# Attention and a two-layer network on one core: batch 0's plain values loaded as four tokens a partition and moved into place by TensorE

## The chip, the core and the metric

The kernel runs on one core of a Trainium2 chip. The metric is the device time of one execution in microseconds; lower is better. Its engines are PE (TensorE, matrix products), ACT (ScalarE), DVE (VectorE), POOL (GpSimd) and SP (SyncE, which here issues nearly all DMAs). PE's results go to PSUM banks; everything else lives in SBUF.

## The reference, cut to what matters

Eight batches of eight heads, 576 tokens, 64 numbers a head. Heads 0 to 3 ("plain") see the last 32 tokens; heads 4 to 7 ("dilated") see every fourth token of the last 128. The result of all heads, 4608 rows of 512, goes through two layers with a leaky ReLU between them.

```python
scores = scale * np.matmul(q, k.transpose(0, 1, 3, 2))
rel = pos[:, None] - pos[None, :]
mask_plain = (rel >= 0) & (rel < 32)
mask_dil = (rel >= 0) & (rel < 128) & (rel % 4 == 0)
attn = softmax(np.where(mask, scores, -1e9))    # plain: heads 0-3, dilated: heads 4-7
x = np.matmul(attn, v).transpose(0, 2, 1, 3).reshape(B * S, H * D)
h = x @ w_in                                    # 512 -> 2048
out = np.maximum(0.01 * h, h) @ w_out           # 2048 -> 512
```

Inputs and output are float32; the kernel works in float16 with float32 sums.

## The kernel before

All steps are written as tasks with their engine (or a choice of engines), a guessed length, what they depend on and a priority. A planner (`_Plan`) goes through them and fixes the order of the instructions on every engine before the kernel is built; `WHEN`, `RANKS`, `MOE`, `SUMS`, `W_SUMS`, `SEEDS` and the guessed lengths steer it. On the chip each engine runs its list in that order and waits where a dependency is not met.

SP's queue of loads in the first phase follows the string `FIRST`, one letter a load or pair of loads: `b` and `v` are batch 0's q with k and its v (dilated heads first, then plain), `c` and `y` are those of batch 1, `i` one eighth of w_in, `o` one eighth of w_out, `0` and `1` the rest (the last 64 tokens) of a batch.

Batches 0 and 1 are computed in two parts. `load_group` loads q, k and v of four heads, and `cast` tasks (on POOL, DVE or ACT) bring them to float16: `nat` for q and k, `v_all` for v. `turn` lets PE transpose q and k into a PSUM bank (`tp`, and `fps` for batch 0's k) and copies them into `slots`. `unit` does a score (PE, with the mask added by a matmul with `ident`, into `sps` or `hps`), its exp (ACT, `ee`), the product with the values (PE, from `v_all` into `ops` or `hps`), log and exp of the sums (ACT, `rc`) and a norm (DVE) that writes `xt`. `load_rest` does the remaining tokens as a second part. Later batches go through `late_unit`.

A plain score of 96 queries takes 128 keys, from 32 ahead of the first query on. So a plain v tile holds 128 tokens on 128 partitions, the next tile starts 96 tokens later, and each head has six tiles. In the kernel before, all six are loaded in that form for batch 0, so that each token of 64 numbers (256 B) is a run of its own; the 32 partitions ahead of the first token are cleared.

`up` does the first layer for a chunk of 384 columns of `xt` (16 blocks of 128 rows of h, each four matmuls, then a leaky ReLU on ACT into `gt`). Chunk 0 is batch 0's first 384 tokens; chunk 1 is batch 1's. `down` does the second layer for the first four tiles of 128 rows, in four quarters of four matmuls into one of two `fps` banks, which DVE copies out. Later tiles go by `group`, in groups of four with seven products in place of eight; `weight_sums` prepares the sums of w_out for this. Up to a planned time of `WARM`, matmuls on `warm` (fillers) are put where the planner sees PE idle and a bank free.

Of the kernel before, what the change touches and what calls it, by code (L numbers as in the profile page):

```python
# [9 lines left out]
FP16 = mybir.dt.float16  # L10
FP32 = mybir.dt.float32
# [17 lines left out]

def _constants():  # L30
# [180 lines left out]
def kernel(  # L211
# [10 lines left out]
    nc = tc.nc  # L222
# [11 lines left out]
    HS = S * D  # L234
    EARLY = 2
    TILED = ((0, 0), (1, 0))
    BY_PE = ((0, 0), (1, 0))
    POOL_MASK = (1,)
    WIDE = (2, 3, 4, 5, 6)
# [185 lines left out]
    def load_group(b, g, prio, prio_v):  # L425
# [28 lines left out]
        if dil and early:  # L454
            lv = [load("SP", at(vs, 0, 128, 0, [256, 4], [1, 256]),
                       dram(v, base, [4 * D, 128], [HS, 4], [1, 256]), 512, 1024, v_old, prio_v)]
            v_late[b] = vs, v_old, v_users
        elif dil:
            lv = [[load("SP", at(vs, 64 * h, 64 * h + 64, 256 * i, [S, 2], [1, 256]),
                        dram(v, base + 2 * h * HS + 256 * i * D, [4 * D, 64], [HS, 2], [1, 256]),  # L460
                        128, 1024, v_old, prio_v) for i in range(2)] + [
                   load("SP", at(vs, 64 * h, 64 * h + 64, 512, [S, 2], [1, D]),
                        dram(v, base + 2 * h * HS + 512 * D, [D, 64], [HS, 2], [1, D]),
                        128, 256, v_old, prio_v)] for h in range(2)]
        elif early:
            lv = []
            for j in range(2):
                n = 12 - (first and j == 0)
# [3 lines left out]
                if n < 12:  # L472
                    lj += [load("SP", at(vs, PAD, 128, 0, [1, D]), dram(v, 0, [D, 96], [1, D]),
                                96, 256, v_old, prio_v), t_vz]
# [19 lines left out]
        for j in range(2):  # L494
# [14 lines left out]
            if not early:  # L509
# [8 lines left out]
            c_v = [cast(at(vt, 0, 128, 0, [w, 2], [128, n], [1, D]),  # L518
                        at(vs, 0, 128, h_a, [h_s, 2], [D, n], [1, D]), 2 * n_v,
                        (lv if dil else lv[0] + lv[1]) + d_old, prio_v, W_ENG)]  # L520
            v_users += c_v
# [6 lines left out]
    def load_rest(b, prio):  # L528


        _, r_old = ring("REST", 1, r_users := [])
        sn, s_old = ring("STG", NST, s_users := [])
        st, lo = stg[sn], []
        for o, src in ((0, q), (1, k)):
            lo.append(load("SP", at(st, 0, 128, o * 256, [1, 256]),
                           dram(src, b * H * HS + 512 * D, [HS, 8], [4 * D, 16], [1, 256]),
                           128, 1024, s_old, prio))
# [6 lines left out]
        lv = load("SP", spread,  # L544
                  dram(v, (b * H + 4) * HS + 512 * D, [4 * D, 16], [HS, 4], [1, 256]),
                  64, 1024, v_old + [t_vr], prio)
        for vi in (2, 3, 0, 1):
# [7 lines left out]
            visits[b, vi, 1] = rest, [c], r_users, vt, c_v + seen_ones[b, vi], d_users  # L555

    w_in_t, w_out_t = {}, {}

# [103 lines left out]
    def turn(b, hp, part, prio):  # L662
# [11 lines left out]
        if b >= EARLY:  # L674
# [17 lines left out]
                ev.append(c)  # L692

            def turned_by(o, n):
                xn, x_old = ring("X", len(turned), x_users := [])
# [146 lines left out]
    def unit(b, hp, part, u, turned, prio):  # L842
        dil = hp >= 2
        ready, t_users, qb, kb = turned
        na, c_qk, n_users, vt, v_deps, v_users = visits[b, hp, part]
        m, par = divmod(b, 2)
        tiled = (b, part) in TILED
        sk, ok = ("S0", "O0") if b == 0 and part == 0 else ("S", "O")
# [432 lines left out]

    roles = [0, 1]
    last_of = {}
    SUMS = -41.62

    def group(four, acts, at_time, split):

# [193 lines left out]
    def attend(b, part, first, step):  # L1481
# [3 lines left out]
        for n, hp in enumerate((2, 3, 0, 1)):  # L1485
            if part != 1 and n % 2 == 0:
                load_group(b, hp // 2, *(ranks[b, hp // 2, i] if b < EARLY else tick()
                                         for i in (0, 1)))
            got = turn(b, hp, part or 0, first + step * n)
# [8 lines left out]
    for m in range(B // 2):  # L1498
# [11 lines left out]
                attend(b, None, a, (z - a) / 4)  # L1510
        x_free[m + 2] = first_ups if m == 0 else []
        if m == 0:
            rings["OSB"] = [[] for _ in range(NO)] + [sum(rings["VST"][i::NVS], []) for i in range(NVS)]
# [107 lines left out]
```

## Time and profile before

| | us |
|---|---|
| median of three runs | 306.18 (306.05 to 307.26) |
| the profiled execution | 307.09 |
| its span | 305.2 |
| PE busy | 293.0 (96%) |
| DVE busy | 249.9 (82%) |
| ACT busy | 225.1 (74%) |
| POOL busy | 118.8 (39%) |

The span runs from the first to the last instruction of the profiled execution; the execution's own time is 1.9 us longer. Busy time is the union of an engine's rows. Consecutive matmuls overlap in it, so a busy PE can still be short of its pace. The granted clock of PE was 0.997 of full speed.

### The profile page before, as it was taken

To read this page: it belongs to the slowest core of one execution; us is meant where nothing else is said; L and a number is where in the kernel's file an instruction comes from. 1 tells how busy PE (TensorE), PEld (TensorE's weight loads), DVE (VectorE), ACT (ScalarE), POOL (GpSimd) and SP (SyncE) were. 2 spreads that over 40 slices of the span, in tenths; PEclk is the share of its full clock that TensorE was granted. 3 is DMA by queue.
4 is the path that set the end of the run, shared out by engine and by line. 5 is a ranking of instruction groups with operands and counts; after the bars stand their busy time and mean duration, and the time that the engine had idled before them with its cause. 6 is when DMAs were issued, how large, how long until landed. Compare 5 with 4: busy or idle time off the path is not lost.

```text
span 305.2 us, 8114 instructions
## 1 busy us (share of the span) xinstructions
PE 293.0 (96%) x3039; PEld 230.5 (76%) x3039; DVE 249.9 (82%) x477; ACT 225.1 (74%) x549; POOL 118.8 (39%) x164
## 2 busy tenths in 40 slices
PE   8788889999999999999999999999999999999994
PEld 4444544566898778778777787778999999999983
DVE  6778785749899989998998899999998868586842
ACT  4989985789898885787677778667568888777420
POOL 6148643058936826936845753771000000000000
PEclk9999999999999999999999999999999999999998
DMA  7999999899799697757994898782212110121034
GB/s 248 336 320 393 312 378 200 171 180 202 173 174 195 134 173 157 138 130 141 177 159 138 148 189 153 143 175 78 73 55 80 42 37 0 37 71 35 11 111 123
DMA packets 157159, 47.22 MB, mean 155 GB/s; under 512 B 137408, under 2 KB 154560, under 8 KB 157120
## 3 DMA queue, kind: packets, MB, share of 16 engines
q1 hardware_dynamic: 156544, 46.39, 64.6%
q8 instruction: 24, 0.39, 0.6%
q10 hardware_dynamic: 576, 0.32, 0.4%
q14 instruction: 15, 0.12, 0.1%
HBM read 37.24 MB, written 9.44 MB: 153 GB/s over the span
## 4 chain that ended last, share of the span: by engine, by line
PE 78%; DVE 6%; ACT 5%; DMA 4%; SPq 3%; issue 1%; DVEq 0%
PE hps L1073 22%; PE fps L1335 21%; PE tp L1335 8%; PE hps L1157 7%; PE fps L1244 5%; PE ops L1016 4%; PE ops L1157 3%; DMA wst<-in_moe_w_in_dram 3%; SPq L333 3%; PE sps L1157 2%; ACT gt L1084 1%; PE sps L1010 1%; PE sps L1016 1%; DVE ee L1026 1%; PE ops L1010 1%
## 5 line engine op out<-in xcount | busy, mean ns | idle before, releaser
L1073 PE MATMUL hps<-xt,w_in 128*128 128x384 f16 (+1 forms) x556 | 97.6, 307 | 1.7 <-DVE w_in L344 1.2
L1335 PEld LDWEIGHTS <-gt 128*128 128x128 f16 x768 | 72.3, 98 | 9.0
L1084 ACT ACTIVATE gt<-hps 128x384 f16<-128x384 f32 (+1 forms) x139 | 62.2, 455 | 22.6 <-PE hps L1073 21.3
L1073 PEld LDWEIGHTS <-w_in 128*128 128x128 f16 x576 | 50.1, 98 | 25.4 <-ACT w_in L342 1.8
L1335 PE MATMUL fps<-w_out,gt 128*128 128x256 f16 x368 | 47.2, 272 | 0.0
L687 POOL COPY slots<-turned 64x512 f16<-64x512 f16 (+1 forms) x36 | 25.7, 715 | 41.2 <-DVE turned L697 34.8
L344 POOL CAST v_all<-vst 64x1152 f16<-64x1152 f32 (+3 forms) x29 | 34.8, 1201 | 7.6 <-DMA vst<-in_v_dram 6.9
L344 POOL CAST nat<-stg 128x576 f16<-128x576 f32 (+1 forms) x44 | 33.8, 789 | 8.0 <-DMA stg<-in_k_dram 3.6
L1026 DVE TENSOR_TENSOR ee<-ee,late_m 128x384 f16<-128x384 f16 (+1 forms) x48 | 29.0, 619 | 3.8 <-ACT ee L1023 3.5
L1045 DVE TENSOR_TENSOR xt<-ops,rc 128x288 f16<-128x288 f32 x48 | 26.5, 553 | 3.7 <-PE ops L1016 2.3
L1157 PEld LDWEIGHTS <-w_in 128*128 128x128 f16 x256 | 21.8, 98 | 0.4
L1364 ACT COPY stg<-fps 128x512 f32<-128x512 f32 (+1 forms) x24 | 12.7, 530 | 11.9 <-PE fps L1335 11.8
L1037 ACT ACTIVATE rc<-rc 128x288 f32<-128x288 f32 x48 | 20.9, 447 | 0.6
L717 DVE STREAM_TRANSPOSE slots<-nat 64x576 f16<-64x576 f16 x24 | 18.4, 767 | 0.4
L697 DVE STREAM_TRANSPOSE turned<-nat 128x576 f16<-128x576 f16 (+1 forms) x24 | 17.5, 735 | 0.4 <-ACT nat L342 0.2
L1157 PEld LDWEIGHTS <-stg 128*128 128x128 f16 x192 | 16.6, 98 | 0.3
L1321 DVE TENSOR_TENSOR gt<-gt 128x1024 f16<-128x1024 f16 x21 | 16.2, 773 | 0.6 <-PE fps L1335 0.6
L1016 PEld LDWEIGHTS <-v_all 128*128 128x128 f16 x240 | 14.5, 98 | 3.0 <-issue 0.2
L1016 PE MATMUL ops<-ee,v_all 128*128 128x96 f16 (+2 forms) x240 | 16.4, 199 | 0.1
L1335 PE MATMUL fps<-wst,gt 128*128 128x256 f16 x128 | 16.4, 273 | 0.0
L967 DVE TENSOR_TENSOR xt<-ops,rc 64x192 f16<-64x192 f32 (+1 forms) x30 | 10.6, 352 | 6.9 <-ACT rc L963 6.4
L1244 PE MATMUL fps<-w_out,gt 128*128 128x512 f16 x64 | 16.1, 380 | 0.0
(151 smaller groups left out, 594.2 us busy)
## 6 DMA issues: line engine op xcount, KB each, us to landing
stg<-in_q_dram SPq DMA_DIRECT2D x48, 144.0 KB, 3.4
stg<-in_k_dram SPq DMA_DIRECT2D x48, 144.0 KB, 3.1
vst<-in_v_dram SPq DMA_DIRECT2D x12, 288.0 KB, 4.1
vst<-in_v_dram SPq DMA_DIRECT2D x24, 128.0 KB, 2.7
gt<-in_moe_w_in_dram SPq DMA_DIRECT2D x5, 512.0 KB, 8.2
xt<-in_moe_w_out_dram SPq DMA_DIRECT2D x3, 512.0 KB, 5.7
gt<-in_moe_w_out_dram SPq DMA_DIRECT2D x3, 512.0 KB, 8.0
vst<-in_v_dram SPq DMA_DIRECT2D x3, 384.0 KB, 6.0
```

The costliest lines, as they stand in the source:

```text
L344: ENG[e].tensor_copy(out=dst, in_=src)
L687: lambda e: (nc.scalar.copy if e == "ACT" else nc.gpsimd.tensor_copy)(out=at(to, p0, p1, p0 if to is qb else 0, *dims), in_=at(fr, p0, p1, ...
L717: lambda e, p0=64 * h: nc.vector.transpose(at(qb, p0, p0 + 64, p0, [128, 9], [1, 64]), na[p0:p0 + 64, S:2 * S]), prio))
L1016: nc.tensor.matmul(at(bk, 0, 128, o, *dims), stationary(s), et[:, c:c + n], start=i == 0, stop=i == len(parts) - 1, skip_group_check=True)
L1026: lambda e: nc.vector.tensor_tensor(out=et[:, 0:w], in0=et[:, 0:w], in1=mk, op=ALU.mult), prio + 0.1)
L1037: lambda e: nc.scalar.activation(out=rt[:, 0:NQ], in_=rt[:, 0:NQ], func=AF.Exp, scale=-1.0),
L1045: lambda e: nc.vector.tensor_tensor(out=dst, in0=at(ot, 0, 128, 0, *src), in1=at(rt, 0, 128, 0, *src), op=ALU.mult), prio + 0.2)
L1073: nc.tensor.matmul(ht[:, 0:n], at(w_in, 0, 128, i * DFF + j // 2 * 256 + j % 2, [2, 128]), at(xt[m % 2], 0, 128, i * 1152 + x0 + x, [1, n] ...
L1084: lambda e: nc.scalar.activation(out=gt[c % NG][:, j * n_c + x:j * n_c + x + n], in_=ht[:, 0:n], func=AF.Prelu, alpha=0.01),
L1157: nc.tensor.matmul(bk[:, 192 * jj:192 * jj + 192], w(i, 2 * jp + jj), x(i), start=first and jj == 0 and i == 0, stop=jj == 1 and i == 1, s ...
L1244: nc.tensor.matmul(ft, g[:, j * n_c + tt * 128:j * n_c + tt * 128 + 128], w_out[:, j * DM:j * DM + DM], start=(j == 0), stop=(j == NJ - 1))
L1335: nc.tensor.matmul(bk[:, x:x + HN], tl[:, off + j * step:off + j * step + 128], rhs(j), start=first and x == 0 and j == 0, stop=j == HJ - ...
```

## The change

For batch 0 (`SEL`), the plain values of the first 512 tokens come in two loads with four consecutive tokens (1 KB) on each partition, into `vst`. Two casts bring them to float16 in `osb[0]`. `pick` is a 128 by 576 matrix in `turned[2]`: zeros, and in every fourth column from the 35th on a single one, in row 0, 1, 2 and so on (the identity matrix, spread out). 128 neighbouring columns of it serve as weights; which ones depends on the tile and on r, the place of the token among the four of its partition. PE so moves token r of each partition to the partition of its key, and four matmuls (r = 0 to 3) add up to one tile of four heads. `pick_values` does this for tiles 0 to 3 (two to a PSUM bank, `sps` or `hps`), and `move` tasks copy them into `v_all`. The missing keys ahead of token 0 come out as zeros. Tiles 4 and 5 of each head are loaded in the old form by `load_rest`, later. The planner's figures and `FIRST` are others, so the order of the instructions differs on all engines: in the queue of loads the near-mask load goes from fourth place to behind batch 1's plain q and k, two loads of w_out come ahead of batch 1's plain q and k, and the others ahead of its plain v.

```diff
-WHEN = (4.52, -1.03, 5.19, 90.96, 96.86, 93.61, 150.56, 174.24)
+WHEN = (31.41, -0.6, 17.98, 85.1, 92.7, 99.49, 158.42, 166.15)
-W_SLOW = 1.25
-SEEDS = (0, 0, 0, 0, 0, 0, 0, 0, 0, 775539)
+W_SLOW = 1.5
+SEEDS = (0, 0, 0, 0, 0, 0, 0, 0, 206472, 469597)
-NEAR = -1498.63
-FIRST = 'bvbviiii0iiiicycyoooooooo1'
-RANKS = ((12.88, -25.12), (25.21, -10.26), (-1.14, 23.42), (33.7, 4.07))
+NEAR = -1482.0
+FIRST = "bvbviiii0iiiicoocoyoooooy1"
+RANKS = ((24.53, -24.71), (34.17, 3.07), (0.12, 16.48), (29.7, 7.1))
...
-    t_vz = clear("POOL", vst[1][0:PAD, 0:D], 0.1, 0.0, -9350)
+    pick = turned[2]
+    t_pick = clear("DVE", pick.bitcast(FP32), 0.34, 0.0, -9440)
+    t_pick = add((("DVE", 0.18), ("ACT", 0.2)), None, 0.2, [t_pick, t_id],
+                 lambda e: (nc.scalar.copy if e == "ACT" else nc.vector.tensor_copy)(
+                     out=at(pick, 0, 128, 35, [4, 128]), in_=ident), -1450)
+    pick_users, flat_v, picked = [], {}, {}
...
+        elif b in SEL:
+            lv = [load("SP", at(vs, 0, 128, 512 * j, [256, 2], [1, 256]),
+                       dram(v, base + 2 * j * HS, [4 * D, 128], [HS, 2], [1, 256]), 256, 1024, v_old, prio_v)
+                  for j in range(2)]
+            v_late[b, "plain"] = vs, v_old, v_users
+            home = osb[0].bitcast(FP16)
+            c_v = [cast(home[:, 512 * j:512 * j + 512], vs[:, 512 * j:512 * j + 512], 512, [lv[j]], prio_v, W_ENG)
+                   for j in range(2)]
+            v_users += c_v
+            flat_v[b] = home, c_v, []
...
+        if b in SEL:
+            ps, p_old, p_users = v_late[b, "plain"]
+            lp = [load("SP", at(ps, 0, 128, 1024 + 256 * i, [D, 4], [1, D]),
+                       dram(v, b * H * HS + (352 + 96 * i) * D, [D, 128], [HS, 4], [1, D]), 512, 256, p_old, prio)
+                  for i in range(2)]
+            for j in range(2):
+                vt, d_users = kept[b, j]
+                c_p = cast(at(vt, 0, 128, 512, [768, 2], [128, 2], [1, D]),
+                           at(ps, 0, 128, 1024 + D * j, [2 * D, 2], [256, 2], [1, D]), 256, lp + d_users, prio, W_ENG)
...
+    def pick_values(b, u, prio):
+        f, c_f, f_users = flat_v[b]
+        sn, s_old = ring("S0", len(banks["S0"]), s_users := [])
+        st = banks["S0"][sn]
+        def pe(e):
+            for i in range(2):
+                x = 35 + 96 * (2 * u + i) - PAD
+                for r in range(4):
+                    nc.tensor.matmul(st[:, 256 * i:256 * i + 256], pick[:, x - r:x - r + 128],
+                                     at(f, 0, 128, r * D, [256, 4], [1, D]), start=r == 0, stop=r == 3,
+                                     skip_group_check=True)
+        t = add("PE", 0.86, 0.25, c_f + [t_pick] + s_old, pe, prio, 0.0, "p")
+        for j in range(2):
+            vt, _ = kept[b, j]
+            m = move(at(vt, 0, 128, 256 * u, [768, 2], [128, 2], [1, D]),
+                     at(st, 0, 128, D * j, [2 * D, 2], [256, 2], [1, D]), 256, [t], prio)
...
-    MOE = 36.21
+    MOE = 36.66
-    W_SUMS = 440.23
+    W_SUMS = 539.34
-    SUMS = -41.62
+    SUMS = -123.87
```

More of the change, by code (lines that the diff above doesn't have):

```diff
@@ L236 @@
     TILED = ((0, 0), (1, 0))
+    SEL = (0,)
     BY_PE = ((0, 0), (1, 0))
@@ L467, in load_group @@
             for j in range(2):
-                n = 12 - (first and j == 0)
+                n = 12
                 lj = [load("SP", at(vs, 0, 128, (12 * j + 12 - n) * D, [D, n], [1, D]),
@@ L517, in load_group @@
             n, w = n_v // D, 128 * (8 if dil else 6)
[L518 to L521, printed above, removed]
+            c_v = []
+            if dil or b not in SEL:
+                c_v = [cast(at(vt, 0, 128, 0, [w, 2], [128, n], [1, D]),
+                            at(vs, 0, 128, h_a, [h_s, 2], [D, n], [1, D]), 2 * n_v,
+                            (lv if dil else lv[0] + lv[1]) + d_old, prio_v, W_ENG)]
+                v_users += c_v
             seen_ones[b, 2 * g + j] = [t_ones["d" if dil else "p", dn]]
@@ L536, in load_rest @@
                            dram(src, b * H * HS + 512 * D, [HS, 8], [4 * D, 16], [1, 256]),
-                           128, 1024, s_old, prio))
+                           128, 1024, s_old, prio, 1.8))
         c = cast(at(rest, 0, 128, 0, [128, 8], [D, 2], [1, D]),
@@ L546, in load_rest @@
                   64, 1024, v_old + [t_vr], prio)
+        if b in SEL:
[7 more added lines that the diff above has]
+                           at(ps, 0, 128, 1024 + D * j, [2 * D, 2], [256, 2], [1, D]), 256, lp + d_users, prio, W_ENG)
+                p_users.append(c_p)
+                picked[b, j, 2] = [c_p]
         for vi in (2, 3, 0, 1):
@@ L555, in load_rest @@
             visits[b, vi, 1] = rest, [c], r_users, vt, c_v + seen_ones[b, vi], d_users
+    def pick_values(b, u, prio):
+        f, c_f, f_users = flat_v[b]
+        f, c_f, f_users = flat_v[b]
+        sn, s_old = ring("S0", len(banks["S0"]), s_users := [])
+        st = banks["S0"][sn]
+        held[st.name].append(s_users)
+        def pe(e):
[6 more added lines that the diff above has]
+        t = add("PE", 0.86, 0.25, c_f + [t_pick] + s_old, pe, prio, 0.0, "p")
+        f_users.append(t)
+        pick_users.append(t)
+        for j in range(2):
+            vt, _ = kept[b, j]
+            m = move(at(vt, 0, 128, 256 * u, [768, 2], [128, 2], [1, D]),
+                     at(st, 0, 128, D * j, [2 * D, 2], [256, 2], [1, D]), 256, [t], prio)
+            s_users.append(m)
+            picked[b, j, u] = [m]
     w_in_t, w_out_t = {}, {}
@@ L694, in turned_by @@
             def turned_by(o, n):
+                if "X" not in rings:
+                    rings["X"] = [[], [], pick_users]
                 xn, x_old = ring("X", len(turned), x_users := [])
@@ L845, in unit @@
         na, c_qk, n_users, vt, v_deps, v_users = visits[b, hp, part]
+        v_deps = v_deps + picked.get((b, hp, u), [])
         m, par = divmod(b, 2)
@@ L1488, in attend @@
                                          for i in (0, 1)))
+            if part == 0 and b in SEL and hp == 0:
+                for u in units:
+                    pick_values(b, u, first + step * n)
             got = turn(b, hp, part or 0, first + step * n)
@@ L1512 @@
         if m == 0:
-            rings["OSB"] = [[] for _ in range(NO)] + [sum(rings["VST"][i::NVS], []) for i in range(NVS)]
+            rings["OSB"] = [flat_v[0][2], [], []] + [sum(rings["VST"][i::NVS], []) for i in range(NVS)]
         while n_c < len(chunks) and chunks[n_c][0] <= m and (m == 3 or n_c not in SEVEN):
```

3 lines of the change are left out of this document (removed).

## The prediction

> **What bounds the kernel now.** I read the busy digits first, then the stages, the chain of waits over the first 50 us, the PE timeline around 50 us and the table of waits.
>
> Part 2 of the page (40 slices of 7.6 us):
>
> ```profile
> PE   8788889999999999999999999999999999999994
> DMA  7999999899799697757994898782212110121034
> ```
>
> PE is full from the seventh slice, about 46 us, to the end. So the span is PE's work plus what PE loses, and most is lost before 46 us. The stages (us, then busy PE, PEld, DVE, ACT, POOL; clock, DMA share, GB/s):
>
> ```profile
> 20.00:30.00 10.00, 8.63 (x64) 4.61 (x65) 8.55 (x21) 8.22 (x19) 8.19 (x12) 1.00 1.05 379
> 30.00:40.00 10.00, 8.68 (x81) 5.13 (x78) 7.92 (x21) 9.80 (x24) 5.77 (x11) 1.00 1.03 317
> 40.00:50.00 10.00, 9.44 (x86) 5.05 (x85) 7.31 (x20) 7.36 (x24) 3.48 (x6) 1.00 1.03 339
> 50.00:60.00 10.00, 9.96 (x71) 5.28 (x70) 6.40 (x13) 6.03 (x15) 1.22 (x2) 1.00 0.85 158
> ```
>
> The DMA engines are full to 50 us, ACT nearly so from 30 to 40 us and with room from 40 on. PE's 8.6 of 10 flatters: a matmul row lasts 0.33 us where the next may start after 0.16, and filler matmuls on `warm` count. The chain of waits (start, us, what) shows what the first stage waits for:
>
> ```profile
> 6.81 2.39 SPq L333
> 9.72 1.78 SPq L333
> 12.49 9.65 DMA wst<-in_moe_w_in_dram
> 22.17 0.34 ACT w_in L342
> ```
>
> The stream of loads carries the chain to 22.14, when the last load of the first half of w_in lands. The end of the first phase, in the PE timeline:
>
> ```profile
> 49.82 0.33 PE L869 MATMUL sps<-con 128*128 128x384 f16 x1
> 50.53 1.90 PE L1244 MATMUL fps<-w_out,gt 128*128 128x512 f16 x8
> 53.52 0.59 PE L1558 MATMUL fps<-warm 128*128 128x512 f16 x2
> 54.82 1.46 PE L1073 MATMUL hps<-xt,w_in 128*128 128x384 f16 x8
> ```
>
> At 49.82 stands the eighth and last score of batch 1's first part, at 54.82 the first up of chunk 1.
>
> **The ledger.** I price matmuls by their steps: 128x512 0.217 us (eight downs in a chain step of 1.83 with its gap), 128x384 0.163, 128x256 0.109. All useful matmuls come to 272.6 us. Those queued ahead of 49.82 make 27.7, so 22.1 are lost by then; at 54.82 it is 32.1 and 22.7. From there to the last matmul at 300.6 another 5.4 go, and 4.6 are the tail to 305.2. The profiled execution took 307.09 with a span of 305.2; the median of the timed runs is 306.18, which is the span plus 1.0. I add that 1.0 to a span.
>
> **Part by part.** *Loads.* The plain values were 3,040 packets of 256 B. In the DMA records 2,981 such packets pass between 10 and 13 us, so 3.06 us. Their place is taken by 512 packets of 1 KB; between 6 and 9 us these pass at 372 per us, so 1.38 us. The near-mask load (128 packets of 20 ns over 16 engines, 0.16 us) moves behind batch 1's plain q and k. The first half of w_in moves up by 1.68 + 0.16 = 1.8 us, to 20.3. SP issues one DMA less here and the mask's issue of 0.47 us goes later; SP's waits are the stream's own. Behind batch 0's rest come the 1,024 packets of 256 B of the late tiles, 1.03 us, so the second half of w_in gains 0.8, and what follows the mask 0.65.
>
> The Trainium skill ("DMA: Bandwidth & Descriptors", Why small descriptors are slow) prices a packet at its 32-byte beats plus three cycles, so 11 and 35 cycles for 256 B and 1 KB. Its estimate for the first saving is 1.4 us; this trace has 18 and 46 ns a packet, a larger ratio, and decides.
>
> *Picks.* 16 matmuls of 128x256 with 16 weight loads: 1.74 us of PE, ahead of the first up, where PE runs 16 fillers after the opening eight and waits besides (3.2 us lost between 15 and 20 us alone). They go into lost time at no cost; without that cover, 1.74. Queued behind them on PE are batch 0's plain scores, since the picks take `sps` and one `hps` and these must be emptied. Two casts of 512 columns (0.61 POOL, 0.62 ACT) and four moves of 256 columns from PSUM replace two casts of 768 (0.84, 0.87). No row is such a move: the 192-column norm takes 0.36, the 512-column eviction 0.68; I take 0.4, nearer the first. The late tiles' casts of 256 columns (0.2 to 0.6, say 0.35, between the casts of 192 to 512) stand on ACT and POOL before the second half of w_in. The ones matrix adds a memset of 0.30 on DVE and a 128-column copy on ACT; neither is before a landing. The late masks leave ACT's early queue (0.97).
>
> *How late are the norms?* Values land at about 12.8, casts end at 13.9, picks at 15.8, moves at 15.9 (`sps`) and 16.8 (`hps`). ACT then alternates exps, logs and casts of w_in, and DVE takes two casts of the third w_in load (18.9) before the last three norms, so the first up starts at about 22.1, against 19.3. The 32 ups of the first half (5.2) and the turn of the rest (0.44) then end at 27.8, against 26.4. What is late next hides it: before, PE stood 1.16 us, until 28.31, for w_in's second half on DVE:
>
> ```profile
> 28.31 0.50 PE L1073 MATMUL hps<-xt,w_in 128*128 128x384 f16 x2 [1.16 <-DVE w_in L344]
> ```
>
> So the norms cost nothing up to a first up at 22.6.
>
> One more wait, on the banks:
>
> ```profile
> DVE slots L648 <- ACT slots L646: 4.9, 8, 0.9
> ACT slots L646 <- DVE slots L648: 3.4, 7, 0.7
> ```
>
> ACT and DVE emptying one bank take turns. `sps` is emptied by both, so 0.4 more before its score: first up at 22.5, inside the cover by 0.1.
>
> The Trainium skill ("PSUM — Partial Sum Buffer", PSUM bank collisions raise a hardware error) says two engines must not touch one bank and quadrant at once; by that rule too the two moves are serial, and the trace agrees (15 such waits).
>
> *Order after 28 us.* This is the largest term. FIRST and the planner's figures put two w_out loads ahead of batch 1's plain q and k, and all w_out loads ahead of its plain values. So downs of chunk 0 slip in among batch 1's scores: ahead of the eighth score stand 31.35 us of useful matmuls, 29.6 without the picks, against 27.7. Downs were held by loads: POOL waited for w_out until 50.13. If batch 1's chain of turns and scores keeps its pace (DVE's queue up to it is the same within 0.6 us, ACT's 1 us shorter), PE has done 1.95 us more by 49.8. POOL's casts of w_out have cover: it is busy 3.5 of 10 us there. DVE's two weight sums of 1.2 come before the first evictions, and tile three's downs wait on those; at that pace the evictions are done first.
>
> *Then.* Ahead of chunk 1's first up stand 38.6 us, so it starts at about 57.6; batch 1's last plain values precede it by 1.7 and their log, exp and norm (0.33, 0.36, 0.36 and gaps) end at 57.2 to 57.8, so I charge 0.1. Before, the same useful work (36.9) was reached at 59.9. Later loss I leave at 5.4 + 4.6; other seeds reorder it, for which I allow 0.8 either way.
>
> Sum: -1.95 + 0.1 = about -1.9. Span 303.3, median **304.3**.
>
> **Rivals.** *Stream only.* Batch 1's chain of scores moves back by as much as downs come forward, since its values land later and DVE holds the casts. For it: DMA is full to 50 us, and bytes hardly change. Against it: those values land at 47 to 50 (they take the place of the last w_out loads, which POOL got at 47.5 and 50.1), and PE wants them at about 52.7 (34.3 us queued ahead). Then only the 0.65 us stays: 305.5.
>
> *Slower: norms behind weights.* DVE and ACT queue casts of the third w_in load ahead of chunk 0's last norms. If that load lands at 20.7 as before, norms end at about 23.8 and the first up starts at 24.1, 1.5 past the cover. Everything of chunk 0 follows, the early downs too, so nothing comes forward: 305.2 + 1.5 + 1.0 = 307.7. For it: DVE runs in order, and the walk leaves 0.1 to 0.5 of cover. Against it: stream and packets speak for 18.9. It decides from a first up at 22.6.
>
> *The loads do not speed up.* If 1 KB packets of this load pass no faster by bytes than the old ones, w_in gains 1 us at most and the late packets take it back; with the picks hidden, 306.3. Against it: the same form of load for q and k passes at 372 packets per us.
>
> **How the numbers follow.** Downs forward, 0.50, giving 304.3, by itself 303.2 to 305.3; stream only 0.24; norms behind weights 0.18; no faster loads 0.08. About 0.5% (1.5 us) is what a measurement of this kernel can tell from no change. The first case lies beyond it in 0.44 of its 0.50; the second and fourth are within it but for 0.03 between them, 0.01 faster and 0.02 slower; the third is slower. So faster 0.45, same 0.35, slower 0.20. The range goes from the first case with another 0.8 of later loss saved and 0.7 more of early, 302.8, to the slower rival, 307.7.
>
> **What would show it.** Right: the last first-half w_in load lands near 20.3; the first up is near 22; fewer fillers after it (8 are queued, 15 before); chunk 1's first up near 57.6; loss after it near 10. Wrong: a first up after 22.6 with DVE's last norms behind `w_in<-wst`; batch 1's eighth score well after 50; or a later stage (DVE around 100 us) that loses more than the 5.4.

## The result, and the profile after

| | before | after |
|---|---|---|
| median of nine runs each, us | 306.39 (305.72 to 307.26) | 307.49 (307.00 to 308.01) |
| ratio to before | | 1.0036, 95% interval 1.0022 to 1.0050 |
| the profiled execution, its span | 307.09, 305.2 | 307.5, 305.7 |
| PE, DVE, ACT, POOL busy | 293.0, 249.9, 225.1, 118.8 | 293.6, 247.8, 223.9, 123.2 |

The changed kernel is slower by 0.36%, 1.1 us, where 304.3 had been forecast. The two profiled spans differ by 0.5 only, since the profiled execution of before was itself 0.7 above its median.

The slices of the page of after, to be held against those of before:

```profile
PE   8788899899999999999999999999999999999994
DMA  7999988799897897848794988791211310031034
```

PE comes to 9 in the sixth slice, one earlier than before, and falls back to 8 in the eighth (53 to 61 us). The DMA engines drop to 8, 8 and 7 in the sixth to eighth slices, one digit under before. The stages, with the same columns as before (us, then busy PE, PEld, DVE, ACT, POOL; clock, DMA share, GB/s):

```profile
20.00:30.00 10.00, 9.00 (x68) 4.87 (x68) 7.72 (x23) 9.09 (x25) 6.34 (x10) 1.00 1.03 379
30.00:40.00 10.00, 8.89 (x81) 5.53 (x81) 7.42 (x18) 9.60 (x22) 7.39 (x13) 1.00 1.05 405
40.00:50.00 10.00, 9.29 (x82) 5.36 (x80) 7.64 (x22) 7.92 (x24) 6.05 (x12) 1.00 0.86 208
50.00:60.00 10.00, 9.10 (x71) 4.44 (x70) 6.95 (x15) 5.58 (x17) 0.33 (x1) 1.00 0.77 156
```

From 30 to 40 us 405 GB/s pass in place of 317, and from 40 us on the engines that load have time to spare (0.86 in place of 1.03): the stream is ahead. PE, however, is busy 9.10 of the ten us from 50 to 60, where it had been 9.96. POOL's row (start, length, engine and line, what, idle time and what ended it) shows when the last of the four loads of the first half of w_in landed:

```profile
18.26 0.74 POOL L345 CAST w_in<-wst 64x512 f16<-64x512 f32 x1 [1.27 <-DMA wst<-in_moe_w_in_dram]
```

It is there at 18.26, 3.9 us before its time in the kernel before and 2.0 before the forecast. PE around the end of the first phase, in the timeline:

```profile
14.49 1.05 PE L596 MATMUL sps<-osb,turned 128*128 128x256 f16 x8 [1.41 <-ACT osb L343]
...
22.04 0.33 PE L1128 MATMUL tp<-xt,w_in 128*128 128x384 f16 x1
22.64 0.74 PE L1128 MATMUL tp<-xt,w_in 128*128 128x384 f16 x3 [0.28 <-DVE xt L1022]
...
46.81 0.59 PE L1299 MATMUL fps<-w_out,gt 128*128 128x512 f16 x2 [0.57 <-DVE w_out L345]
...
51.32 0.33 PE L924 MATMUL sps<-con 128*128 128x384 f16 x1
...
58.94 0.38 PE L1616 MATMUL fps<-warm 128*128 128x512 f16 x1
60.18 0.33 PE L927 MATMUL sps<-slots 128*128 128x96 f16 x4 [0.86 <-ACT ee L949]
60.35 1.46 PE L1128 MATMUL hps<-xt,w_in 128*128 128x384 f16 x8
```

The picks start at 14.49, the first up at 22.04, batch 1's eighth score at 51.32 (49.82 before), chunk 1's first up at 60.35 (54.82 before, 57.6 forecast). PE loses time at two places on the way: around 46 us, where it runs three fillers (45.00) and then stands for DVE's cast of w_out, and from 58.94 to 60.18, where it has one filler to do and then waits 0.86 us for an exp of batch 1's rest.

**The ledger over time.** The forecast's ledger, carried on: time lost up to t is t less the useful matmuls that started before t, each at the forecast's price for its columns; picks and fillers are not useful work, so all kernels have 272.6 us of it. One profiled execution each. Five kernels (after, e9, e13, e14, e15) have the same order up to 70 us; their loss at 65 us lies between 23.02 and 23.56, so a difference under 0.5 says little in this table. The six kernels without after's early order (before, e2, e5, e7, e11, e12) lie between 22.4 and 22.9 there.

| lost by (us) | 25 | 45 | 55 | 65 | 80 | 90 | 110 | 290 |
|---|---|---|---|---|---|---|---|---|
| before | 13.8 | 21.5 | 22.6 | 22.9 | 23.1 | 23.4 | 24.9 | 27.9 |
| after | 15.6 | 20.2 | 21.6 | 23.4 | 23.5 | 25.1 | 26.2 | 29.0 |
| e7 (before's start, after's later order) | 13.6 | 21.2 | 22.4 | 22.7 | 23.0 | 25.1 | 26.2 | 29.1 |
| e11 (picks, before's later order) | 16.1 | 21.6 | 22.6 | 22.7 | 23.0 | 23.3 | 24.8 | 27.7 |
| e10 (after, picks done twice) | 16.9 | 21.6 | 23.1 | 24.6 | 24.8 | 26.4 | 27.4 | 30.3 |

After is 1.8 us behind at 25 us (late norms), 1.3 ahead at 45 (downs come early), and 0.5 behind again at 65. A second loss, 1.6 us, falls between 80 and 90, of which before loses 0.3; before loses somewhat more behind it, so that the two are 1.3 us apart at 110 and 1.1 at 290.

### The profile page after: what moved, and what is told of

Read it like the earlier page. It is cut to its first block, busy times and chain, and to the rows that moved or that the text cites. A ratio compares the mean times of both kernels' runs of the same rounds, so it can differ in the third digit from the quotient of the medians.

```text
span 305.7 us, 8137 instructions
## 1 busy us (share of the span) xinstructions
PE 293.6 (96%) x3050; PEld 231.4 (76%) x3050; DVE 247.8 (81%) x480; ACT 223.9 (73%) x547; POOL 123.2 (40%) x170
## 4 chain that ended last, share of the span: by engine, by line
PE 78%; ACT 10%; DVE 7%; DMA 2%; issue 2%; SPq 1%; ACTq 0%
PE hps L1128 22%; PE fps L1390 21%; PE tp L1390 8%; PE hps L1212 7%; PE ops L1071 4%; PE ops L1212 3%; PE fps L1299 3%; DMA stg<-in_q_dram 2%; ACT gt L1139 2%; PE sps L1212 2%; ACT slots L698 2%; ACT ee L949 2%; ACT rc L1016 1%; DVE ee L1081 1%; PE sps L1071 1%
## 5 line engine op out<-in xcount | busy, mean ns | idle before, releaser
L1139 ACT ACTIVATE gt<-hps 128x384 f16<-128x384 f32 (+1 forms) x139 | 62.9, 457 | 21.8 <-PE hps L1128 20.3
L1128 PEld LDWEIGHTS <-w_in 128*128 128x128 f16 x576 | 49.9, 98 | 22.3 <-issue 1.7
L739 POOL COPY slots<-turned 64x512 f16<-64x512 f16 (+1 forms) x36 | 27.7, 769 | 42.8 <-DVE turned L751 30.3
L345 POOL CAST v_all<-vst 64x1152 f16<-64x1152 f32 (+4 forms) x30 | 35.2, 1175 | 8.8 <-DMA vst<-in_v_dram 8.4
L345 POOL CAST nat<-stg 128x576 f16<-128x576 f32 (+1 forms) x46 | 34.9, 783 | 6.9 <-DMA stg<-in_q_dram 3.3
L1081 DVE TENSOR_TENSOR ee<-ee,late_m 128x384 f16<-128x384 f16 (+1 forms) x48 | 27.1, 575 | 3.8 <-ACT ee L1078 3.2
L1092 ACT ACTIVATE rc<-rc 128x288 f32<-128x288 f32 x48 | 21.2, 449 | 0.5
L1419 ACT COPY stg<-fps 128x512 f32<-128x512 f32 (+1 forms) x25 | 13.4, 534 | 10.6 <-PE fps L1390 10.2
L1071 PE MATMUL ops<-ee,v_all 128*128 128x96 f16 (+2 forms) x240 | 16.4, 199 | 0.6 <-DVE xt L1100 0.6
L1390 PE MATMUL fps<-wst,gt 128*128 128x256 f16 x128 | 16.4, 272 | 0.0
L1071 PEld LDWEIGHTS <-sides 128*128 128x128 f16 x240 | 13.8, 97 | 3.0 <-issue 0.3
L1390 PE MATMUL tp<-w_out,gt 128*128 128x256 f16 x120 | 15.6, 273 | 0.0
```

Of the source, the lines that this page charges most:

```text
L345: ENG[e].tensor_copy(out=dst, in_=src)
L739: lambda e: (nc.scalar.copy if e == "ACT" else nc.gpsimd.tensor_copy)(out=at(to, p0, p1, p0 if to is qb else 0, *dims), in_=at(fr, p0, p1, ...
L1071: nc.tensor.matmul(at(bk, 0, 128, o, *dims), stationary(s), et[:, c:c + n], start=i == 0, stop=i == len(parts) - 1, skip_group_check=True)
L1081: lambda e: nc.vector.tensor_tensor(out=et[:, 0:w], in0=et[:, 0:w], in1=mk, op=ALU.mult), prio + 0.1)
L1092: lambda e: nc.scalar.activation(out=rt[:, 0:NQ], in_=rt[:, 0:NQ], func=AF.Exp, scale=-1.0),
L1128: nc.tensor.matmul(ht[:, 0:n], at(w_in, 0, 128, i * DFF + j // 2 * 256 + j % 2, [2, 128]), at(xt[m % 2], 0, 128, i * 1152 + x0 + x, [1, n] ...
```

## The experiments

**Figures and structure apart.** The change has two halves: the structure (tokens, picks, late tiles) and the planner's figures. e1 gives the kernel before the figures of after, e2 gives the changed kernel those of before (`WHEN`, `FIRST`, `W_SLOW`, `SEEDS`, `NEAR`, `RANKS`, `MOE`, `W_SUMS`, `SUMS` and a lateness of 1.8 us planned for one load), and e3 and e4 take from each its drawn orders (`SEEDS`).

```diff
e1 (before), and the reverse of it in e2 (after):
-WHEN = (4.52, -1.03, 5.19, 90.96, 96.86, 93.61, 150.56, 174.24)
+WHEN = (31.41, -0.6, 17.98, 85.1, 92.7, 99.49, 158.42, 166.15)
-FIRST = 'bvbviiii0iiiicycyoooooooo1'
+FIRST = "bvbviiii0iiiicoocoyoooooy1"
...
e3 (after) and e4 (before):
+SEEDS = (0, 0, 0, 0, 0, 0, 0, 0, 0, 0)
```

> The kernel before with the changed kernel's planner figures and queue of loads, without picks: 24 downs ahead of batch 1's eighth score and 48 ahead of chunk 1, as in the changed kernel (12 and 28 before). Theory 'order': the loss of 1.1 us is made by the order, since the downs pulled forward hold up batch 1's last values and chunk 1's first up (60.35 against 54.82), so this one is 0.5 to 1.5 us slower than before. Theory 'picks': the loss is made by the picks' chain ahead of chunk 0's last norms, so this one is as fast as before or up to 1 us faster, with chunk 1's first up by 58.5.

> The changed kernel with the planner figures and the queue of loads of before: picks, 1 KB loads and late tiles as in the change, but 12 downs ahead of batch 1's eighth score and 32 ahead of chunk 1. Theory 'order': as fast as before or faster by up to 0.7 us (the loads end earlier, the picks lie in lost time). Theory 'picks': slower by 0.7 to 1.5 us, first up near 22 and the loss already there at 35 us.

> The changed kernel with all ten planner passes without random moves. If the loss in the stage from 80 to 90 us (1.57 us lost there, 0.29 before) is a matter of the drawn order, it moves or goes and the time changes by 0.5 us or more; if it belongs to the change, it stays within 0.4 us of the changed kernel.

> The kernel before with all ten planner passes without random moves: how much a drawn order is worth without any change in the work. Theory 'drawn orders': 0.5 to 1.5 us slower than before, as large as the change's whole loss. Else within 0.4 us.

Measured: e1 312.55 us, ratio 1.0221 (1.0187 to 1.0256). e2 307.37, 1.0038 (1.0019 to 1.0057). e3 309.56, 1.0111 (1.0079 to 1.0144). e4 309.33, 1.0109 (1.0075 to 1.0142). The figures of after are no gain by themselves: on the old structure they cost 6.5 us, 3.3 of it by 65 us in the ledger, where neither theory of e1 had expected more than 1.5. Without drawn orders the two kernels cannot be told apart; the draw takes 3.3 us off before (its median in this call is 306.0) and 2.1 off the changed kernel (307.49), so the difference between them seems to come with the draw. Four runs each leave about 0.9 us either way, however, so this pair alone does not show it. e2's time lies in the range of theory 'picks', its loss does not lie where that theory put it: e2 puts 32 downs ahead of chunk 1's first up in place of 48, is 0.2 to 0.5 ahead of before from 60 to 95 us in the ledger, and ends 1.2 behind it, lost in later stages whose order the planner made anew.

So three theories stood from here on. A: the early downs only borrow, and what they win by 55 us goes back by 65. B: the rest of the loss is the order of the later steps and has nothing to do with the picks. C, the rival: the picks and the late norms behind them come through to the end.

**Orders joined at a time.** A table holds one kernel's complete order; the planner's own is followed up to a planned time (chip time is about 2 us more), then the table's.

```diff
     order.sort(key=lambda t: (t.start, t.n))
+    done = [t for t in order if t.start < 68]
+    early = set(id(t) for t in done)
+    for n, e in zip(LATER, LATER_ON):
+        t = plan.tasks[n]
+        if id(t) not in early:
+            t.eng = {"P": "PE", "A": "ACT", "D": "DVE", "G": "POOL", "S": "SP"}[e]
+            done.append(t)
...
+    order = done
```

| run | start from | until | then the order of |
|---|---|---|---|
| e5 | picks with before's figures (e2) | 68 | before |
| e6 | after | 72 | before |
| e7 | before | 72 | after |
| e11 | e2 | 47 | before |
| e12 | e2 | 82 | before |

> The first 70 us are those of the changed structure planned with the figures of before (four tokens a partition, picks on PE, 32 downs ahead of chunk 1's first up), everything after them is before's own order, engine for engine. In the kernel whose first part this is, the time lost had been 0.24 us under before's at 65 us and 0.30 us under it at 85 us. Theory B (the later stages' drawn order costs what is lost after 70 us): that lead is kept, 305.5 to 306.3 us, 0.1 to 0.5 under before. Theory C (the picks and the norms behind them reach the end, later): about 1.0 us slower than before, 307.0 to 307.6, with the loss growing between 100 and 240 us as in that kernel.

> The changed kernel's order up to about 74 us, before's order from there. Theory A (what the earlier downs win by 55 us is given back by 65, 0.5 us too much, and the stage around 80 to 90 us is a second, separate loss of the later order): 0.5 us slower than before, 306.6 to 307.1, with the loss at 65 us near 23.4 and no step of 1.2 us between 85 and 90. Theory C (all of it comes through from the start): 1.1 us slower, as the changed kernel.

> Before's order up to about 74 us, the changed kernel's from there. Theory A and B (the later order has a loss of its own, 0.6 us): 306.7 to 307.2, with a step of about 1.2 us in the loss between 85 and 90 us, half of it given back by 110. Theory C (the loss is the start's): equal to before within 0.2 us.

> The four tokens a partition and the picks in the order planned with the figures of before up to 49 us, then before's order; no PE work changes sides at the seam, and 28 downs stand ahead of chunk 1's first up, as in before. Theory B (nothing of the loss comes from the loads, the picks or the late norms): within 0.4 us of before, 305.8 to 306.6, with the loss at 60 us within 0.3 of before's 22.85. Theory C: 0.7 us or more slower.

> As the early-picks kernel with before's late order, but with the seam at about 84 us in place of 70. There a group of four downs that had been taken ahead left its place empty, and ups waited at 73.5 and 75.4 us, 1.3 us in all. With the seam later that loss should be gone: loss at 80 us near 22.8 as in the kernel with picks alone, at 110 near before's 24.9 less 0.2 to 0.4, and the time 305.6 to 306.2, ahead of before if anything is. If the stages behind 84 us take back any lead (what comes early waits for DVE there): 306.1 to 306.7, equal to before.

Measured: e5 306.59 us, ratio 1.0016 (0.9998 to 1.0033). e6 309.23, 1.0088 (1.0065 to 1.0111). e7 307.34, 1.0034 (1.0014 to 1.0055). e11 306.38, 1.0009 (0.9993 to 1.0026). e12 307.11, 1.0026 (1.0010 to 1.0042).

e11 is the cleanest: no PE work changes sides at its seam, it has the four-token loads, the picks and the late tiles, and its time cannot be told from before's. Its interval reaches up to 0.8 us, just into theory C (0.7 or more); what puts theory C out is the ledger. The first up is at 22.23, and 2.3 us more than in before are lost at 25 us, yet at 55 us the two are level, and they stay so to the end. e7 has nothing of the change but its order from 74 us on and is as slow as the changed kernel. It reaches 80 us 0.5 ahead of after and stands level with it at 90: that stage takes as much more from it as it had won. In both kernels PE stands at the same steps: at 85.25, 86.06 and 88.41 in after, at 85.35, 86.17 and 88.52 in e7. (Some 2 us of PE work changes sides at e7's seam, so its size is less sure than its place.) The windows of DVE in the stage (columns as above; before, after, e11, e7 in that order):

```profile
66.00:78.00 12.00, 12.00 (x113) 8.28 (x112) 10.51 (x22) 11.33 (x30) 10.59 (x16) 1.00 1.01 183
78.00:92.00 14.00, 14.00 (x195) 13.00 (x193) 12.59 (x21) 12.19 (x37) 7.92 (x9) 1.00 0.83 170
```

```profile
66.00:78.00 12.00, 12.00 (x98) 8.08 (x96) 8.39 (x19) 10.26 (x25) 9.27 (x12) 1.00 1.05 193
78.00:92.00 14.00, 13.45 (x195) 12.25 (x194) 13.87 (x23) 11.90 (x40) 6.45 (x8) 1.00 0.92 180
```

```profile
66.00:78.00 12.00, 12.00 (x114) 8.34 (x113) 10.38 (x22) 11.16 (x30) 10.58 (x16) 1.00 1.06 195
78.00:92.00 14.00, 14.00 (x196) 13.02 (x194) 12.62 (x21) 12.47 (x37) 7.78 (x9) 1.00 0.80 162
```

```profile
66.00:78.00 12.00, 12.00 (x100) 8.19 (x99) 9.88 (x20) 9.47 (x24) 10.59 (x16) 1.00 1.04 196
78.00:92.00 14.00, 13.01 (x185) 11.53 (x184) 13.55 (x23) 10.97 (x36) 5.84 (x7) 1.00 0.84 166
```

The fifth column is DVE. With before's later order it works 10.4 to 10.5 us of the first window and 12.6 of the second, and PE never stands. With after's it works 8.4 (or 9.9) of the first and then 13.6 to 13.9 of 14, and PE stands. The 1.0 to 1.3 us by which DVE is busier in the second window are no more than the same work lasting longer beside POOL's casts: its two products of 384 columns with the mask took 0.69 us together in before, 1.74 in after and 1.26 in e7, and its sum over 2048 elements 1.51, 1.98 and 1.95.

e6 came out 2.1 us above its range. It loses 1.8 us from 75 to 80, right behind its seam, and then 0.8 from 80 to 90, where after loses 1.6 and before 0.3. So the one run with after's start and before's later order agrees on the place but cannot tell what that start is worth. e5 and e12 show as well why such seams must be read with care: in e5 a group of downs that before has at 74.14 had been run already, and the ups around its empty place waited for ACT:

```profile
73.55 0.49 PE L1269 MATMUL hps<-xt,w_in 128*128 128x192 f16 x4 [0.25 <-ACT gt L1280]
...
75.44 0.82 PE L1269 MATMUL hps<-xt,w_in 128*128 128x192 f16 x8 [0.38 <-ACT gt L1280]
```

e5's loss goes from 22.3 at 70 us to 23.6 at 80 there. e12 passes that place without loss (22.5 at 80) and loses 1.6 from 85 to 100 us, behind its own seam, where before loses 1.0. Neither beats before: e5's time lies between the ranges of its two theories, and e12 is 0.4 above the higher of its two. So that a lead of 0.5 us at 70 us can be kept to the end was not shown by any run.

**The stall before chunk 1.** e8 moves ten steps of batch 1's rest behind the norms of the tiles ahead of it.

```diff
     order.sort(key=lambda t: (t.start, t.n))
+    behind = [t for t in order if t.n in BEHIND]     # eight copies, a score, its exp
+    order = [t for t in order if t.n not in BEHIND]
+    spot = 1 + max(i for i, t in enumerate(order) if t.n == 396)     # the last norm
+    order[spot:spot] = behind
```

> The changed kernel with ten steps of batch 1's last tile (the eight copies of turned plain values, their first score and its exp) put behind the norms of the tiles before it, so that nothing stands ahead of those norms on ACT and DVE. Chunk 1's first up, at 60.34 us in the changed kernel, comes near 59.1. Theory A (the norm's lateness is what takes back the gain): 0.8 to 1.2 us faster than the changed kernel, 306.3 to 306.7. Rival (the copies are needed soon anyway and the loss moves to the rest's scores, or the end is set by later stages): within 0.4 us of the changed kernel, with the loss back at its level by 65 to 70 us.

Measured: 309.16 us, ratio 1.0100 (1.0065 to 1.0136), 1.7 slower than after, so both theories missed. DVE's norms came 0.8 earlier (58.73 in place of 59.53), but two scores of the rest stand ahead of chunk 1's first up in PE's order, and those now waited for the copies. In the timeline of e8:

```profile
60.52 0.34 PE L929 MATMUL sps<-slots 128*128 128x96 f16 x4 [1.31 <-DVE slots L702]
61.86 0.33 PE L929 MATMUL sps<-slots 128*128 128x96 f16 x4 [1.00 <-ACT ee L951]
62.03 1.46 PE L1130 MATMUL hps<-xt,w_in 128*128 128x384 f16 x8
```

The expectation named the wrong step: in after, too, the wait of 0.86 us at 60.18 is for the rest's exp. That exp and chunk 1's last norms end together (60.13 and 60.15), so to bring one of them forward is not enough. The lag passed to the end here: 1.4 us behind after at 65, 1.5 at 290.

**Are the picks hidden?** e10 does each pick twice.

```diff
-                for r in range(4):
-                    nc.tensor.matmul(st[:, 256 * i:256 * i + 256], pick[:, x - r:x - r + 128],
+                for again in range(2):
+                    for r in range(4):
+                        nc.tensor.matmul(st[:, 256 * i:256 * i + 256], pick[:, x - r:x - r + 128],
...
```

> The changed kernel with each of its picks done twice (the second pass starts its sum anew, so the values are the same): 1.74 us more of PE between 14 and 18 us, ahead of chunk 0's norms. What the prediction said of the picks (they lie in time that PE loses anyway, and the ups' cover reaches from 22.1 to 22.6): chunk 0's first up goes from 22.04 to 22.9 to 23.8 and the time rises by 0.0 to 0.5 us, to 307.5 to 308.0. Rival C (norms that come late push everything behind them): up by 0.9 to 1.7 us, 308.4 to 309.2.

Measured: 309.40 us, ratio 1.0109 (1.0087 to 1.0132), so 1.9 above the changed kernel for 1.74 us of added PE work: rival C's side, and 0.2 over its range. The first up moved from 22.04 to 23.48, and the ledger ends 1.3 behind after. The first 1.74 us of picks were covered (e11), the second are not. That agrees in kind with the forecast's edge, a first up at 22.6, beyond which lateness would cost; the cost is more than the 0.9 us by which 23.48 lies beyond it.

**The stage from 78 to 92 us.** PE's steps that stand in after:

```profile
85.25 0.33 PE L1071 MATMUL ops<-ee,v_all 128*128 128x96 f16 x5 [0.30 <-DVE xt L1100]
86.06 0.36 PE L1065 MATMUL sps<-slots 128*128 128x96 f16 x5
88.41 0.35 PE L1071 MATMUL sps<-ee,sides 128*128 128x96 f16 x5
```

By the ledger's prices 0.47, 0.30 and 0.28 us are lost just ahead of them. Where before has the same kind of steps, it has groups of downs between them:

```profile
84.94 1.03 PE L1335 MATMUL fps<-w_out,gt 128*128 128x256 f16 x8
87.03 1.03 PE L1335 MATMUL fps<-w_out,gt 128*128 128x256 f16 x8
```

After has no group from 83.6 to 91.5. DVE's rows of after:

```profile
80.23 1.98 DVE L1329 TENSOR_TENSOR w_out<-w_out 128x2048 f16<-128x2048 f16 x1
82.50 1.66 DVE L1081 TENSOR_TENSOR ee<-ee,late_m 128x384 f16<-128x384 f16 x2
84.78 0.41 DVE L1100 TENSOR_TENSOR xt<-ops,rc 128x288 f16<-128x288 f32 x1
```

PE's wait at 85.25 is for the norm at 84.78. Four runs tried to give the stage its time back: e9 puts the sum at 80.23 behind four norms, e15 gives it to POOL, e13 and e14 move groups of downs (0.87 us of PE each) from ahead of the stage's waits into or behind them.

```diff
e15 (e9 has task 734 in place of 815, and not the second edit):
+    fold, = [t for t in order if t.n == 611]
+    order.remove(fold)
+    spot, = [i for i, t in enumerate(order) if t.n == 815]
+    order.insert(spot + 1, fold)
...
-            t_sum[n] = shared("DVE", 1.16, 0.2, deps, lambda e: nc.vector.tensor_tensor(
+            t_sum[n] = shared("DVE", 1.16, 0.2, deps, lambda e: (nc.gpsimd if n == 3 else nc.vector).tensor_tensor(
e13 (pairs: a task, and the one that it is put behind; 616 to 619 are the groups):
+BEHIND = ((627, 773), (619, 584), (618, 578), (626, 726), (617, 562), (616, 546))
e14:
+BEHIND = ((627, 773), (619, 584), (618, 578))
```

> The changed kernel with one step moved: DVE's sum over 2048 elements of w_out, 1.98 us at 80.23 us ahead of four norms, goes behind the fourth of them (it is wanted by PE only near 91.5 us). Theory D (after 78 us DVE sets the pace, without idle time, and that sum stands ahead of what PE wants): the loss between 80 and 90 us falls from 1.57 to 0.2 to 0.8 us and the time to 306.4 to 306.9. Theory B in its wide form (it is the order of the stage as a whole; PE has 20 more chunk-0 downs behind it and too little left to put between batch 2's waits): the loss moves to the waits behind the sum's new place, and the time stays within 0.4 us of the changed kernel's 307.5.

> The changed kernel with four groups of eight 256-wide downs (0.87 us of PE each) put later among PE's steps, with the two copies that follow them: the group at 71.19 us goes behind the first scores of batch 2, the others behind later ups, the last two behind the places where PE waits for norms at 85.25 and 87.20. Theory A2 (downs that run early are cover taken from a later wait; batch 2's first scores, at 75.53, stand behind one of them): the scores come 0.9 us earlier, DVE's idle 1.56 us at 75.1 shrinks, the loss from 80 to 92 us falls from 1.6 to 0.3 to 0.9, and the time goes to 306.4 to 307.0. Rival (the loss belongs to the order of the other engines, whatever PE puts between): within 0.4 us of the changed kernel's 307.5.

> The same with the last two groups alone, from 81.18 and 82.71 us to behind 84.6 and 87.4. PE's work ahead of 91 us is the same in sum and batch 2's first scores keep their place, so if DVE sets the pace from 78 us on nothing changes but the names of the waits: 307.2 to 307.8. If what counts is only that a group stands beside each wait: 306.6 to 307.0.

> The changed kernel with the sum over 2048 elements of w_out that DVE does at 80.23 us (1.98 us) given to POOL, which stands idle from 84.7 to 93.0 us; at POOL's 0.91 us for 384 elements of such a sum in the trace of before it would take some 4.9 us, from 84.7 to 89.6, ahead of its use at 91.54. Theory D2 (in the stage from 78 to 92 us DVE has more work than time, 13.87 of 14.0 us against 12.59 in before, so that work has to leave it, not to change place): PE's loss from 80 to 92 us falls from 1.6 to 0.3 to 1.0 us, the time to 306.4 to 307.0. Rival (DVE's steps beside POOL's sum get longer by as much, as its own sum beside POOL's cast took 1.98 us in place of 1.18): 307.2 to 308.0.

Measured: e9 307.82 us, ratio 1.0055 (1.0036 to 1.0074). e13 310.44, 1.0121 (1.0091 to 1.0150). e14 309.53, 1.0097 (1.0067 to 1.0128). e15 307.33, 1.0034 (1.0013 to 1.0055). None recovers the loss; e9 and e15 came out as their rivals had it. Without the sum in front the waits of e9 move behind its new place (start 88.04, 1.21 us):

```profile
89.59 0.34 PE L1071 MATMUL ops<-ee,sides 128*128 128x64 f16 x5 [0.57 <-DVE ee L1081]
```

In e15 POOL did the sum in 4.07 us, from 83.51 on (4.9 expected), and DVE is still busy 13.03 of 14 us from 78 to 92; one product with the mask, 0.94 us in place of 0.37, lasts longer beside it, and PE waits for that product:

```profile
86.87 0.94 DVE L1081 TENSOR_TENSOR ee<-ee,late_m 128x416 f16<-128x416 f16 x1
```
```profile
87.87 0.35 PE L1071 MATMUL sps<-ee,sides 128*128 128x96 f16 x5 [0.60 <-DVE ee L1081]
```

Its ledger is better than after's by 0.5 from 90 us on, but by 0.4 already at 65, where the two orders are the same; its time is better by 0.16, which its interval cannot tell from nothing. e14 shows what the two groups at 81.18 and 82.71 had been covering:

```profile
82.88 0.33 PE L1073 MATMUL ops<-ee,v_all 128*128 128x96 f16 x5 [0.30 <-DVE xt L1102]
83.73 0.33 PE L1073 MATMUL sps<-ee,sides 128*128 128x96 f16 x5 [0.52 <-DVE ee L1083]
85.49 0.33 PE L1073 MATMUL ops<-ee,v_all 128*128 128x96 f16 x5 [0.59 <-DVE xt L1102]
```

PE came to those steps 1.7 us sooner and stood there for 1.4. From 80 to 85 us it loses 1.9 us, after 0.4; from 85 to 95 the two lose the same (1.4 and 1.3), although the groups now lie there. e13 loses 1.8 more than after by 110 us in the same way. Both theories fell for these two runs: moved behind the waits, the groups of downs saved nothing, and where they had stood they had covered 1.5 of their 1.74 us. The two runs did not put a group where before has one, however: e14's came to stand at 89.17 and 91.61 (its expectation had said behind 84.6 and 87.4), and e13's at 76.06, 81.67, 88.65 and 91.09.

What is settled is the place: the order of the later steps, at 80 to 92 us, while DVE is full. That DVE's load is the cause is not shown, and which steps would have to stand elsewhere is open: four attempts by hand did not find it. That the order lacks groups of downs between PE's waits from 85 to 88 us is a rival that no run tested by itself.

## Why the prediction was wrong, point by point

The forecast's own ledger of the span was 272.6 of work, what is lost by chunk 1's first up, a later loss and the tail. Before: 22.7, 5.4 and 4.6. Forecast for after: 20.8 and the other two as they were. Measured: 37.2 us of useful work lie ahead of the up at 60.35, so 23.1 are lost by then; the last matmul at 301.6 leaves 5.9 for later; the tail is 4.1. The miss of 2.4 us in the span is 2.3 in the first term, 0.5 in the second and -0.5 in the tail. In the median it is 3.2: the forecast put the median 1.0 above the span, since the profiled execution of before took 0.9 us more than the median, and the median of after is 1.8 above its span.

- *Order after 28 us, -1.95: the step that failed.* Its condition, that batch 1's chain of scores keeps pace, did not hold. The eighth score came at 51.32 instead of 49.8, with the forecast's 29.6 us of work ahead of it: 21.7 lost in place of 22.1, so 0.4 of the 1.95 was won there. The lead had been larger: 1.3 at 45 us. It went around 46 us (20.2 lost at 45, 21.5 at 47.3), where PE ran three fillers and stood for DVE's cast of w_out. Of the 2.3 us, 1.5 were gone by the eighth score and 0.8 between it and chunk 1's first up.
- *Chunk 1's first up, +0.1.* It came 2.7 us later than forecast, because PE had emptied its downs by 59 and stood for batch 1's rest. The log, exp and norm that were to end at 57.2 to 57.8 ended at 60.15: ACT did four copies of the rest's turn, by turns with DVE, ahead of the logs (58.70). The outcome is that of the rival "stream only" (the chain moves back by as much as downs come forward), which gave 305.5, but half of its reason fails. DVE's casts did hold PE (0.57 us at 46.81); late values did not, since the products with the values at 54.41 and 57.15 started with 0.09 us lost ahead of each. With e2 and e11 (32 and 28 downs ahead, loss 22.6 and 22.7 at 65 us) beside after (48 downs, 23.4), it looks as if the early downs were borrowed, not won; these kernels differ in their other figures too, so the downs alone are not isolated.
- *Later loss, left at 5.4 with 0.8 either way.* 5.9 in the ledger, inside that allowance; that it makes the forecast's 10.0 together with the tail is luck, 0.5 more of the one and 0.5 less of the other. The term had the wrong weight: e7 shows that this term alone makes the changed kernel as slow as it is, whatever the start. So the early lead, had it come, might have been lost there. The text named "a later stage that loses more" among the things that would make it wrong; it came at 80 to 92 us, not at 100.
- *Loads: right in kind, too small.* From 6 to 24 us 6.86 MB pass in 4,704 packets, against 6.08 MB in 5,930. The last first-half load of w_in landed 3.9 us earlier, not 1.8. Part of that is the w_in packets themselves: from 13 to 16 us 308 packets of 4 KB pass in after, of 159 ns on average, and 245 of 202 ns in before; why they were slower there is not shown. The forecast's "larger ratio" holds by the byte (four packets of 18 ns against one of 46 is 1.57, four of 11 cycles against one of 35 is 1.26), not by the packet. Nothing was won by the earlier landing, since the first up waited for norms.
- *Picks, norms, first up.* Forecast 15.8 for the end of the picks and 22.1 (22.5 with turn-taking) for the first up; measured 16.4 and 22.04. Hidden in the end (e11), and twice the picks are too much (e10), but the cover did not lie where the forecast had it, in the wait that ended at 28.31: at 28 us after is still 0.8 behind before, and level with it only at 38; e11 is 1.8 behind at 28 and level at 55. ACT's cast into `osb` started only at 13.82, behind copies that took turns with DVE, so the picks began at 14.49.
- *Slower rival, norms behind weights.* Its condition did not occur, and its 307.7, close to the measured 307.49, was reached by another way.
- *Bound for a difference.* The 1.1 us are under the 0.5% that the text took as the least that can be told; the interval of nine runs each is narrower than that.

## What to carry to other kernels

Work that is pulled forward into one wait may be taken from the cover of a later one: before counting it as won, price the wait that it used to hide. A change that comes with a new searched order has two effects; join the old order to the new structure (and the new order to the old structure) at a point where nothing changes sides, and the two come apart. A search's order is worth about 1% here, more than the change it is fitted to, so a structural gain of under 1% is not read from two searched kernels.

## What the runs showed of the hardware

- The same sum over 2048 elements took DVE 1.98 us in after and 1.51 in before, both beside POOL's casts of `vst`, 1.21 in e9 with POOL idle, and POOL 4.07 in e15.
- DVE's products with the mask (two operands in SBUF) got longer beside POOL's work as well: two in 1.66 us at 82.50 in after, beside POOL's casts, where one at 87.98 took 0.37 with POOL idle. The first of the two ended at 83.43, 0.21 after the cast that POOL had begun before it (81.19 to 83.22); in e15 the one that started at 86.87 ended at 87.81, 0.23 after POOL's sum (83.51 to 87.58). DVE's transposes (0.76 to 0.79 in both) and norms from PSUM (0.41 to 0.46) did not. The Trainium skill ("SBUF — State Buffer", SBUF: two separate sides) has a rule for it: a DVE operation with two SBUF inputs and a POOL operation that reads SBUF share one pair of ports, and whichever starts first holds it to its end. The traces agree, and by that rule work given from DVE to POOL comes back in part as waits of DVE.
- A DMA packet's time went with its bytes plus a fixed part: in before, packets of 4, 256, 1024 and 4096 bytes took 9, 18, 46 and 159 ns (medians of the DMA records, 4 to 16 us), which is 9 ns and some 37 ns a KB.
- Copies that ACT and DVE do in turn from one PSUM bank held up the steps queued behind them on both: ACT's cast into `osb` started at 13.82, 2.1 us behind its twin on POOL (11.74), and four such copies at 56.39 to 58.67 stood ahead of batch 1's last logs (58.70).
